# Flags of a chunk-selecting attention: PSUM to the score operands without a DMA between

## The chip, the cores and the metric

The kernel runs on one core of a Trainium2 chip. The time is device microseconds of one launch; the kernel before took 357.41 us (median of 3 runs, 354.07 to 358.31). The profile is of one further execution, whose span from the first to the last instruction is 337.3 us. Engines: PE multiplies matrices and transposes, ACT, DVE and POOL work on vectors, SP issues DMAs. DMAs copy between HBM and SBUF, or from SBUF to SBUF. PE writes to PSUM, which ACT and DVE read.

## The reference

An attention layer that keeps six chunks of keys per query, followed by a dense two-layer network plus a mixture of eight experts, of which each row takes one. Only the attention is touched by the change. Cut:

```python
# q, k, v: (4, 8, 768, 64); chunks of 32 keys, 24 of them
k_min, k_max = min and max of each chunk of k
ub = sum over d of max(q * k_min, q * k_max)          # a bound for each query and chunk
ub = where(chunk not later than the query's own, ub, -1e9)
top_chunks = argsort(ub)[..., -6:]                    # the six chunks kept
scores = q @ k.T / sqrt(64)
scores = where(chunk of the key in top_chunks and key not after query, scores, -1e9)
attn = softmax(scores)
out = attn @ v
# then, on (3072, 512): relu(x @ w1) @ w2, plus gate * relu(x @ w1[e]) @ w2[e] for the row's expert e
```

## The kernel before

Heads are worked on in 16 pairs. A pair's operands of the score matmul are two tiles of K and two of Q, each 128 partitions by 768 positions, in three rotating sets (`NB = 3`). The contraction runs over the 128 partitions, and the mask is folded into it: half of the partitions hold the 64 head dimensions, and part of the other half holds, on K's side, -30000 where a key lies in chunk c (`exf`), and on Q's side a flag that is 1 where the query does not keep chunk c. So the product already contains -30000 for each key that is not selected.

- head 0: `k0[0:64]`, `r0[0:64]` are K and Q; `k0[64:96]`, `r0[64:96]` are chunk table and flags.
- head 1: `k1[64:128]`, `r1[64:128]` are K and Q; `k1[0:32]`, `r1[0:32]` are chunk table and flags.

Rows left over are zero on one side of the product. The steps for one pair, cut:

```python
def prep_k(p):      # transposes of K on PE, ACT copies both heads to k1, chunk max and min on DVE
    pk = pprep.tile([128, S], HF, name="pp")          # PSUM, two buffers shared by all "pp"
    ...
    nc.scalar.copy(k1, pk)                            # L384
    for i, op in enumerate((ALU.max, ALU.min)):
        nc.vector.tensor_reduce(out=ks[:, i], in_=k1 in chunks, op=op, ...)      # L388
    ... kb = ks times masks of the two heads                                     # L391, L393

def prep_kt(p):
    nc.sync.dma_start(out=k0[0:64], in_=k1[0:64])     # L397, K's second copy
    nc.sync.dma_start(out=k1[0:32], in_=exf[0:32])    # L398

def prep_q(p):
    ... transposes of Q to pq (PSUM)                  # L405
    nc.scalar.activation(qp, pq, AF.Relu)             # L408
    nc.vector.tensor_copy(r0, pq)                     # L409, all 128 partitions
    nc.sync.dma_start(out=r1[64:128], in_=r0[64:128]) # L410, Q's second copy

def prep_ub(p):
    ... bounds of all chunks by matmul (PSUM)         # L416, L420
    ... nc.vector.max per 128 queries and head        # L426, the eight largest
    flags = fl[p % 2]...[:, :, :, 0:NC]
    nc.vector.tensor_tensor(flags, ub, sixth largest, ALU.is_lt)                 # L428

def prep_s(p):
    ps = pprep.tile([128, S], HF, name="pp")
    for t in range(NT):
        nc.tensor.transpose(ps[:, t * 128 : (t + 1) * 128], fl[p % 2][:, t], ident)   # L434
    se = ahead.tile([128, S], HF, name="se")
    nc.vector.tensor_copy(se, ps)                     # L436
    r0, r1 = rT[p % NB]
    nc.sync.dma_start(out=r0[64:96], in_=se[64:96])   # L438
    nc.sync.dma_start(out=r1[0:32], in_=se[0:32])     # L439

def scores(p, u):   # 11 units per pair
    sp = psc.tile([128, 512], FP, name="sp")          # PSUM, three buffers
    ... nc.tensor.matmul(sp[...], kT[p % NB][g][...], rT[p % NB][g][...])        # L448
    nc.scalar.activation(ex, sp, AF.Exp, scale=0.125) # L452
    ... on the diagonal: nc.gpsimd.affine_select(ex)  # L454
```

`fl` has 128 columns per block of queries: 24 flags in columns 0 to 23, 24 in columns 64 to 87, the rest zero since the start of the kernel. After the transpose they stand on partitions 0 to 23 (head 1) and 64 to 87 (head 0), which are the partitions where `r1` and `r0` want them.

The loop over pairs calls these steps between the units of earlier pairs (`n1` is the next pair, `n2` the one after it):

```python
if u == 2: prep_s(n1)
if u == 4: prep_k(n2)
if u == 5: prep_q(n2)
if u == 7: prep_kt(n2)
if u == 9: prep_ub(n2)
... fills: parts of the dense network of the batch before (L242 to L331)
... finish: products with V (L467), division by the row sums (L476, L478)
if u == 0: cast_v(n2); load v of pair p + 4; load an expert's weights
if u == 7: cast_qk(p + 3); load k and q of pair p + 5
```

The scheduler orders the instructions of each engine from these calls; it waits wherever one step reads or overwrites what another writes or reads.

Of the kernel before, what the change touches and what calls it, by code (L numbers as in the profile page):

```python
# [10 lines left out]
HF = mybir.dt.float16  # L11
# [6 lines left out]
def kernel(  # L18
# [12 lines left out]
    nc = tc.nc  # L31
    B, H, S, D = q.shape
# [323 lines left out]
    with (  # L356
# [73 lines left out]
        def prep_s(p):  # L430
            s = st[p]
            ps = pprep.tile([128, S], HF, name="pp")
            for t in range(NT):
                nc.tensor.transpose(ps[:, t * 128 : (t + 1) * 128], fl[p % 2][:, t], ident)  # L434
            se = ahead.tile([128, S], HF, name="se")
            nc.vector.tensor_copy(se, ps)  # L436
            r0, r1 = rT[p % NB]
            nc.sync.dma_start(out=r0[64:96], in_=se[64:96])  # L438
            nc.sync.dma_start(out=r1[0:32], in_=se[0:32])  # L439

        def scores(p, u):
            s = st[p]
# [52 lines left out]
        load(2, "v")  # L495
        load(3, "v")
        prep_s(0)
        prep_k(1)
        prep_q(1)
# [22 lines left out]
        for i, (p, u) in enumerate(seq):  # L522
# [4 lines left out]
            if u == 2 and n1 is not None:  # L527
                prep_s(n1)
# [220 lines left out]
```

## Time and profile before

| | |
|---|---|
| time, median of 3 | 357.41 us |
| span of the profiled execution | 337.3 us |
| busy: PE, DVE, ACT, POOL | 244.4, 165.7, 173.6, 154.0 us |
| DMA | 66.23 MB, mean 196 GB/s |
| `rT<-se` (L438, L439) | 32 transfers of 48 KB |
| `kT<-kT` (L397), `rT<-rT` (L410) | 16 each of 96 KB |
| mean granted PE clock | 0.912 |

A line such as `PE sp L448` names the engine, the tile written and the source line. "DMA rT<-se" is a transfer into tile `rT` from tile `se`. SPq is SP's issuing of DMAs. In the list of waits the engine on the left stood idle until the one on the right released it. The granted clock is a share of full speed, and the DMA share is the mean busy share of the 16 DMA engines; it counts packets, which may overlap, and so can pass 1.

### The profile page before, as it was taken

What the parts mean: (1) busy time and instruction counts of PE and PEld (TensorE: products, weight loads), DVE (VectorE), ACT (ScalarE), POOL (GpSimd) and SP (SyncE); (2) the same over time, 40 slices, a digit from 0 to 9 for tenths busy, and PEclk for the clock granted to TensorE, in tenths of its full rate; (3) what the DMA queues carried; (4) which work ended last, traced back from release to release, by engine and by line L of the source; (5) the groups of instructions that cost most, each with busy time, mean ns of one, the idle gap of its engine ahead of it and who ended that gap; (6) DMA issues with size and microseconds to landing.
All of it is one profiled execution on the core that took longest, in us unless ns stands there. A gap on an engine that the chain in (4) does not pass through costs nothing.

```text
span 337.3 us, 7413 instructions
## 1 busy us (share of the span) xinstructions
PE 244.4 (72%) x2615; PEld 156.8 (46%) x2615; DVE 165.7 (49%) x556; ACT 173.6 (51%) x322; POOL 154.0 (46%) x203
## 2 busy tenths in 40 slices
PE   1418727849949859686686696989874998899882
PEld 1316516628616637454453473655441554444441
DVE  5526606527934447494352586237522454444441
ACT  4318707828817737558373664772341444444441
POOL 6635615436323514443424230110446677777753
PEclk9999958769978969799897989899995999999999
DMA  7976989797998798899994897223869578877760
GB/s 202 276 166 157 185 184 192 143 224 178 195 251 209 180 224 188 176 313 198 248 238 132 151 159 249 76 92 106 277 164 293 171 238 233 244 243 257 227 214 0
DMA packets 80499, 66.23 MB, mean 196 GB/s; under 512 B 30222, under 2 KB 73742, under 8 KB 80464
## 3 DMA queue, kind: packets, MB, share of 16 engines
q1 hardware_dynamic: 65280, 37.17, 40.2%
q0 software_dynamic: 15184, 28.60, 37.8%
q8 instruction: 21, 0.34, 0.4%
q14 instruction: 14, 0.11, 0.1%
HBM read 50.62 MB, written 20.91 MB: 212 GB/s over the span
## 4 chain that ended last, share of the span: by engine, by line
DMA 38%; PE 31%; issue 8%; DVE 8%; POOL 6%; ACT 4%; SPq 3%; POOLq 1%; ACTq 0%; DVEq 0%
DMA rT<-se 24%; PE sp L448 10%; DMA xg<-xd,gi 9%; PE yp L326 6%; POOL xg L647 3%; ACT ex L452 3%; DMA kT<-kT 3%; PE hp L317 3%; PE op L467 2%; POOL out_dram L695 2%; PE yp L691 2%; SPq L88 2%; PE hp L674 2%; PE pp L434 1%; DVE ks L388 1%
## 5 line engine op out<-in xcount | busy, mean ns | idle before, releaser
L452 ACT ACTIVATE ex<-sp 128x512 f16<-128x512 f32 (+1 forms) x176 | 92.6, 591 | 66.3 <-PE sp L448 63.0
L448 PE MATMUL sp<-rT,kT 128*128 128x128 f16 (+3 forms) x384 | 72.3, 297 | 46.8 <-DMA rT<-se 45.7
L454 POOL TENSOR_SCALAR_AFFINE_SELECT ex<-ex 128x512 f16<-128x512 f16 x48 | 31.8, 665 | 84.1 <-ACT ex L452 83.8
L448 PEld LDWEIGHTS <-kT 128*128 128x128 f16 x384 | 32.0, 109 | 56.3 <-issue 50.9
L467 PE MATMUL op<-v,ex 128*128 128x65 f16 x672 | 52.2, 201 | 8.0 <-ACT ex L452 4.7
L467 PEld LDWEIGHTS <-ex 128*128 128x128 f16 x672 | 39.7, 103 | 24.0 <-ACT ex L452 8.5
L695 POOL DMA_INDIRECT out_dram<-yo,si x31 | 31.4, 1013 | 16.0 <-DVE yo L694 9.3
L685 ACT COPY ehT<-tp 128x512 f16<-128x512 f16 x31 | 18.1, 585 | 36.9 <-PE tp L683 36.9
L388 DVE TENSOR_REDUCE ks<-kT 128x24 f16<-128x768 f16 x32 | 29.1, 947 | 14.7 <-ACT kT L384 13.9
L647 POOL DMA_INDIRECT xg<-xd,gi x31 | 29.8, 963 | 12.3 <-issue 5.8
L674 PE MATMUL hp<-we,exT 128*128 x124 | 31.8, 379 | 4.6 <-DVE exT L668 3.3
L691 PE MATMUL yp<-we,ehT 128*128 x124 | 32.7, 387 | 0.8 <-ACT ehT L685 0.8
L426 DVE MAX8 m<-pp 128x8 f32<-128x8 f32 (+4 forms) x160 | 16.0, 167 | 29.1 <-PE pp L420 28.9
L668 DVE COPY exT<-tp 128x512 f16<-128x512 f16 x31 | 13.1, 424 | 33.3 <-PE tp L666 33.3
L326 PE MATMUL yp<-wd,hT 128*128 128x512 f16 x96 | 28.9, 427 | 0.7 <-DVE ys L223 0.6
L317 PE MATMUL hp<-xT,wd 128*128 128x384 f16 x128 | 27.0, 330 | 1.1 <-ACT hT L319 0.3
L436 DVE COPY se<-pp 128x768 f16<-128x768 f16 x16 | 8.9, 557 | 37.3 <-PE pp L434 37.3
L694 DVE SCALAR_TENSOR_TENSOR yo<-yp,xg 128x512 f32<-128x512 f32 x27 | 20.3, 751 | 13.8 <-PE yp L691 12.0
L677 ACT ACTIVATE eh<-hp 128x512 f16<-128x512 f32 x31 | 18.5, 597 | 14.1 <-PE hp L674 14.1
L371 POOL CAST q<-qf 128x768 f16<-128x768 f32 x16 | 13.2, 824 | 25.9 <-DMA qf<-in_q_dram 19.0
L319 ACT ACTIVATE hT<-hp 128x384 f16<-128x384 f32 x32 | 15.8, 495 | 13.2 <-PE hp L317 7.5
L376 POOL CAST v<-vf 128x768 f16<-128x768 f32 x16 | 13.2, 827 | 17.5 <-PE op L467 12.8
(123 smaller groups left out, 386.0 us busy)
## 6 DMA issues: line engine op xcount, KB each, us to landing
we<-in_moe_w_dram POOLq DMA_DIRECT2D x16, 512.0 KB, 8.1
kf<-in_k_dram SPq DMA_DIRECT2D x32, 192.0 KB, 4.1
qf<-in_q_dram SPq DMA_DIRECT2D x32, 192.0 KB, 4.5
vf<-in_v_dram SPq DMA_DIRECT2D x32, 192.0 KB, 5.3
xd<-ys SPq DMA_DIRECT2D x24, 256.0 KB, 3.0
xo<-xbig SPq DMA_DIRECT2D x4, 792.0 KB, 6.7
xd<-xbig SPq DMA_DIRECT2D x4, 792.0 KB, 8.0
kT<-kT SPq DMA_DIRECT2D x16, 96.0 KB, 4.6
```

What stands on the lines that cost most here:

```text
L317: nc.tensor.matmul(hp, wd[:, ko, j * 128 : (j + 1) * 128], xT[:, ko, g * G * 128 : (g + 1) * G * 128], start=(ko == 0), stop=(ko == NK - 1))
L326: nc.tensor.matmul(yp, hold["h"][:, j, i * 128 : (i + 1) * 128], wd[:, NK + j], start=(j == 0), stop=(j == NK - 1))
L388: nc.vector.tensor_reduce(out=ks[:, i], in_=kp.rearrange("d (c w) -> d c w", w=32), op=op, axis=mybir.AxisListType.X)
L448: nc.tensor.matmul(sp[:, o : o + w], kT[p % NB][g][:, kt * 128 : (kt + 1) * 128], rT[p % NB][g][:, a * 128 : z * 128], start=(o == 0), sto ...
L452: nc.scalar.activation(ex[:, 0:o], sp[:, 0:o], AF.Exp, scale=0.125)
L454: nc.gpsimd.affine_select(out=ex, in_=ex, compare_op=ALU.is_ge, fill=0.0, base=0, pattern=[[0, 4], [1, 2], [2, 64]], channel_multiplier=-1)
L467: nc.tensor.matmul(s["op", g][:, t * (D + 1) : (t + 1) * (D + 1)], ex[:, o : o + 128], v16[p % NB][:, g, kt, :], start=first, stop=(last_o ...
L647: nc.gpsimd.indirect_dma_start(out=dst, out_offset=None, in_=src, in_offset=bass.IndirectOffsetOnAxis(ap=gi[:, i : i + 1], axis=0))
L674: nc.tensor.matmul(hp, s["xT"][:, ko], wef[:, bass.ds(offs[i] + ko * 512, 512)], start=(ko == 0), stop=(ko == NK - 1))
L691: nc.tensor.matmul(yp, s["hT"][:, j], wef[:, bass.ds(offs[i] + (NK + j) * 512, 512)], start=(j == 0), stop=(j == NK - 1))
L694: nc.vector.scalar_tensor_tensor(o, yp, s["x"][:, Dm : Dm + 2].bitcast(FP), s["y"], ALU.mult, ALU.add)
L695: sc = nc.gpsimd.indirect_dma_start(out=out, out_offset=bass.IndirectOffsetOnAxis(ap=si[:, i : i + 1], axis=0), in_=o, in_offset=None, bou ...
```

## The change

The tile `se` and its two transfers go. DVE copies the transposed flags from PSUM into the two score operands directly, in two instructions of 64 partitions. The copies cover the whole half (64 rows in place of 32); the added rows are the zero columns of `fl`. Only K's second copy, the chunk table and Q's second copy are still moved by DMA. It is meant to take a transfer from SBUF to SBUF, and its latency, out of the way from flags to scores.

```diff
             ps = pprep.tile([128, S], HF, name="pp")
             for t in range(NT):
                 nc.tensor.transpose(ps[:, t * 128 : (t + 1) * 128], fl[p % 2][:, t], ident)
-            se = ahead.tile([128, S], HF, name="se")
-            nc.vector.tensor_copy(se, ps)
             r0, r1 = rT[p % NB]
-            nc.sync.dma_start(out=r0[64:96], in_=se[64:96])
-            nc.sync.dma_start(out=r1[0:32], in_=se[0:32])
+            nc.vector.tensor_copy(r0[64:128], ps[64:128])
+            nc.vector.tensor_copy(r1[0:64], ps[0:64])
```

In the changed kernel the two copies are L436 and L437, and every later line stands two lines higher (the scores are L446).

## The prediction

> **What bounds the kernel now.** I read the page first (shares of busy time, chain that ended last), then the waits, then the chain in order of time, then the stretches. No engine is saturated: PE is busy 72% of the span and every other engine about half. The chain says where the rest goes.
>
> ```profile
> PE 244.4 (72%) x2615; PEld 156.8 (46%) x2615; DVE 165.7 (49%) x556; ACT 173.6 (51%) x322; POOL 154.0 (46%) x203
> ...
> DMA rT<-se 24%; PE sp L448 10%; DMA xg<-xd,gi 9%; PE yp L326 6%; POOL xg L647 3%; ACT ex L452 3%; DMA kT<-kT 3%; PE hp L317 3%; PE op L467 2%; POOL out_dram L695 2%; PE yp L691 2%; SPq L88 2%; PE hp L674 2%; PE pp L434 1%; DVE ks L388 1%
> ```
>
> The first entry of the chain by line, 24% of 337.3 us = 81 us, is the transfer that the change removes: `rT<-se`. The list of waits gives the time in which PE really stood still for it, and what else stood behind it:
>
> ```profile
> ACT ex L452 <- PE sp L448: 63.0, 26, 8.3
> PE sp L448 <- DMA rT<-se: 45.7, 13, 7.3
> DVE se L436 <- PE pp L434: 37.3, 13, 7.6
> POOL q L371 <- DMA qf<-in_q_dram: 19.0, 7, 5.7
> ```
>
> Columns are total us, times, longest. 13 of the 16 head pairs made PE wait, 45.7/13 = 3.5 us each; ACT's 63 us in front of the exponential and DVE's 37 us in front of the `se` copy lie behind the same wait. One turn of the loop in the chain (start, length in us):
>
> ```profile
> 184.74 0.35 PE pp L434 x6
> 185.12 0.56 DVE se L436
> 185.70 5.85 DMA rT<-se
> ...
> 191.69 0.38 PE sp L448 x4
> ```
>
> The flags of pair p+1 are transposed (L434), copied (L436), sent by DMA (L438, L439), and only then can the scores of pair p+1 start (L448). The transposes of p+2 in turn stand in PE's queue behind scores of p+1. So the transfer is in a ring, paid once per pair. Its time from issue to landing:
>
> ```profile
> DMA to landing us min/median/max: 1.9/5.4/10.6
> ```
>
> By stage (columns: length, then busy us and instruction counts of PE, PEld, DVE, ACT, POOL, the granted clock, DMA share, GB/s):
>
> ```profile
> 24.00:207.00 183.00, 134.28 (x1759) 96.43 (x1759) 100.86 (x390) 110.28 (x211) 71.05 (x98) 0.87 0.90 200
> 207.00:225.00 18.00, 15.73 (x155) 9.83 (x155) 5.21 (x14) 12.99 (x27) 3.96 (x6) 0.91 0.22 78
> 225.00:337.00 112.00, 88.62 (x652) 46.29 (x650) 48.19 (x112) 43.64 (x77) 65.18 (x66) 0.97 0.66 205
> ```
>
> Attention proper is 24 to 225 us. In its first 183 us PE is busy 134.3 and idle 48.7, nearly all of it the 45.7 us above. The last 112 us (dense layers of the last batch, then the experts) do not touch the flags: the change can gain nothing there.
>
> [...] the trace has 549 to 559 ns for `se`. [...] The clock here is 0.87 from 24 to 207 us against 0.97 later, with waits up to 7.3 us[...].
>
> **The change, part by part.**
> 1. Removed: 32 transfers `rT<-se`, two per pair. On the path that is the 45.7 us of PE standing still. SP also loses two issues per pair (medians 0.80 and 0.59 us, single ones up to 4.9 us), which lets the remaining transfers start sooner. In bytes it is little: 32 x 48 KB = 1.5 MB of 66 MB, so the DMA engines are hardly relieved.
> 2. Changed: one DVE copy of 128x768 (0.56 us) becomes two of 64x768[...]. DVE gains 16 x 0.55 = 8.8 us, to about 106 + 9 of the 201 us from 24 to 225: not a bound. From last transpose to the first operand ready it is now 0.56 us in place of 0.56 + about 5.9; head 0 needs only the first half.
> 3. Moved: DVE now writes `r0[64:128]`, which the transfer of Q's second copy (L410) reads. So the first half copy must wait for that transfer, and DVE, which works in order, would stand with it. L410 lands in 2.1/4.1/6.6 us (min/median/max). Its source is written by L409, and in the compiled order of the changed kernel the flags copy of the same pair comes about a pair later on DVE, 9 us or so. I count this as mostly hidden, exposed where SP is held up in front of L410 by a load that waits for its buffer.
> 4. Reordered: in the compiled order of the changed kernel PE's flag transposes of the next pair stand behind the second head's first scores, and its scores follow soon after (in early pairs: 6 flag transposes, 6 of K, 7 products with V, then the scores). So the distance from flags to scores is under 1 us of PE work: tight, but about the length of the copy.
>
> What the ring costs without the DMA, from durations in the trace: transposes of K 0.50, ACT's copy 0.80, two reductions 2 x 0.94, Q's copy 0.55, the `kb` products 0.37, bound matmuls 0.70, ten maxima 0.90, the flags 0.45, flag transposes 0.35, two half copies 1.11: 7.6 us, and with 0.1 us for each of ten hand-offs (my allowance) 8.6 us per pair. PE's own work per pair: (134.3 + 15.7) us busy over the 201 us, times the present period of 12.86 us (first L438 at 21.05, last at 213.96, 15 periods) = 9.6 us. ACT: (110.3 + 13.0)/201 x 12.86 = 7.9 us. So PE becomes the bound, at 9.6 us at best.
>
> Nothing here runs in a perfect packing: PE and ACT hand each unit to each other in order with three score buffers, and the batch-end stretches (for example 191.5 to 208.7 us, DVE 13.09 of 17.2 us) are thick with small DVE work. I take PE at 89% busy, a choice between its 96% in the densest stretch (73.0 to 86.5 us: 12.96 of 13.5) and its 73% now: 9.6/0.89 = 10.8 us per pair. That saves 15 x (12.86 - 10.8) = 31 us. Seen from the waits: of 45.7 us about a third comes back as waits on ACT, on DVE and on loads. Before the first scores (23.9 us, which waited for a transfer issued at 21.05) I expect up to 2 us, and take 1 us off again for DVE's extra copies in the batch-end stretches, net 0 to 1. The sum is -30.5: 357.4 - 30.5 = 327 us. The timed median stands 18 us above the profiled execution; I carry the saving over in us, not as a ratio.
>
> **The rivals.**
> A. The DMA engines become the bound. Share 0.90 over 12.86 us is 11.6 us of packets per pair; at the highest share seen for a whole pair, 1.10 (152.9 to 165.9 us), that is 10.5 us, at 1.0 it is 11.6. For: POOL already waits 19 us for loads of Q. Against: those waits are largely early, loads are issued more than a pair ahead, and expert weights can come late without harm. Period 11.6: saving 19 us, about 338.
> B. DVE stands at L436 for L410's transfer, and the removed wait comes back on another engine. If it cost 2 us in each of 15 pairs on top of 10.8: about 357. Against it: the distance of some 9 us. I give it 5%, with part of it (338 to 345) more likely than all.
> C. Clean removal: all of the 45.7 us goes[...]. Period near 9.6: about 308 to 312. For: the idle time has almost no other cause. Against: it supposes that no new wait arises.
> D. A wait hidden already. This would need the DMA to run beside other PE work; PE's 45.7 us of idleness say it does not.
>
> **Range and chances.** 8 in 10 between 313 (close to C) and 341 (A, with some of B). Faster by over 2% means under 350.3 us: only a full B or two partial ones miss it, so 0.93; within 2% 0.05; slower 0.02, for an order of instructions worse than I read it.
>
> **What would show it.** Right: no `rT<-se` anywhere; PE's wait in front of L446 (the scores) falls from 46 us to under 10; the stage ends near 195 us; PE busy above 80% in it; two half copies of about 0.55 us each; PE's clock at or above 0.90 in that stage; the last 112 us unchanged. Step 3 is wrong if DVE's wait in front of L436 names the transfer `rT<-rT`; rival A shows as POOL or PE waiting for `qf`, `kf` or `vf`, with a share at 1.0 or more and a period above 11 us. The prediction as a whole is wrong if PE's waits before the scores stay above 25 us, whatever their releaser.

## The result, and the profile after

The changed kernel took 327.74, 329.05, 332.68 and 339.33 us, the kernel before 357.14 us (median of 4, 354.07 to 358.31). Executions more than 1.5% above the fastest of their kernel, here the last two, are left out of the medians and differences from here on. That gives 328.40 us, 28.7 us less; with all four it is 330.87 us, 26.3 less. The ratio is 0.921, its 95% interval 0.910 to 0.931. The prediction was 327 us, 30.5 less.

The first two lines are the page's busy times and its chain by line, of the changed kernel.

```profile
PE 241.8 (74%) x2615; PEld 156.0 (48%) x2615; DVE 174.0 (53%) x572; ACT 174.8 (53%) x322; POOL 154.7 (47%) x203
...
DMA rT<-rT 22%; PE yp L689 7%; PE hp L672 6%; PE sp L446 5%; PE yp L326 5%; PE hp L317 5%; DVE ks L388 3%; PE op L465 3%; POOL out_dram L693 2%; PE tp L664 2%; DVE rT L436 2%; POOL xg L645 2%; DVE rT L437 2%; DMA xg<-xd,gi 2%; PE tp L681 2%
```

`rT<-se` is gone, and in its place at the head of the chain stands another transfer, `rT<-rT`, with nearly the same share. The list of waits (us in total, times, longest) says who stands for it:

```profile
DVE rT L436 <- DMA rT<-rT: 42.7, 14, 7.7
ACT ex L450 <- PE sp L446: 31.1, 26, 5.2
...
PE sp L446 <- DVE rT L436: 17.8, 8, 5.4
...
PE pp L405 <- DVE rT L437: 11.1, 3, 6.6
```

Before, PE stood 45.7 us for a transfer; now DVE stands 42.7 us for one. PE gets only part of it: 17.8 us in front of the scores, and 11.1 us in front of Q's transposes (L405), whose PSUM buffer is free only when the second half copy (L437) is done. The copies themselves, and Q's transfer (from L410):

```profile
L436 DVE COPY rT<-pp x16: 560/561/561, 20.1 to 187.2; 64x768 f16<-64x768 f16 x16
L437 DVE COPY rT<-pp x16: 540/550/550, 20.7 to 187.8; 64x768 f16<-64x768 f16 x16
```
```profile
DMA to landing us min/median/max: 2.6/4.8/6.9
```

The first starts of L436 at 20.1 and the last at 187.2 us make a period of 167.1/15 = 11.14 us per pair, against 12.86 before. One turn of the new ring, from the chain in order of time (start, length):

```profile
32.42 6.95 DMA rT<-rT
39.37 0.03 issue
...
39.46 0.56 DVE rT L436
40.02 0.03 issue
40.05 0.55 DVE rT L437
40.60 1.72 DVE ks L388 x2
42.32 0.47 DVE rT L409
42.78 0.73 DVE kb L391
43.52 0.04 DVE kb L393
43.56 5.58 DMA rT<-rT
```

Of 11.1 us, 7.0 are the transfer. Nearly all other links of this ring are DVE's, in its own order: the copy that must wait for the transfer (L436) holds up the work that starts the next one. The two `kb` links are none: the transfer reads only `r0`, which L409 had finished at 42.8 us. It was issued at 43.6 because SP was still issuing loads of K.

Stages, from the stretches of both profiles. The attention stage ends with the last division by row sums, at 227.2 us before and at 200.1 us now, 27 us earlier:

```profile
24.00:200.00 176.00, 141.62 (x1925) 101.21 (x1922) 115.04 (x421) 124.14 (x238) 74.88 (x103) 0.93 0.94 208
200.00:327.00 127.00, 92.43 (x629) 48.94 (x626) 47.36 (x111) 42.56 (x75) 65.31 (x66) 0.92 0.56 179
```

From there to the end this execution takes 127 us and the one before took 110. The next section shows that this is not the change: in another execution of the same kernel it is 112 us.

### The profile page after: what moved, and what is told of

It reads as the page before. It is cut to its first block, busy times and chain, and to the rows that moved or that the text cites. A ratio compares the mean times of both kernels' runs of the same rounds, so it can differ in the third digit from the quotient of the medians.

```text
span 327.3 us, 7387 instructions
## 1 busy us (share of the span) xinstructions
PE 241.8 (74%) x2615; PEld 156.0 (48%) x2615; DVE 174.0 (53%) x572; ACT 174.8 (53%) x322; POOL 154.7 (47%) x203
## 4 chain that ended last, share of the span: by engine, by line
PE 39%; DMA 27%; DVE 12%; issue 8%; POOL 4%; ACT 4%; SPq 3%; another core or an unknown queue 1%; POOLq 0%; ACTq 0%; DVEq 0%
DMA rT<-rT 22%; PE yp L689 7%; PE hp L672 6%; PE sp L446 5%; PE yp L326 5%; PE hp L317 5%; DVE ks L388 3%; PE op L465 3%; POOL out_dram L693 2%; PE tp L664 2%; DVE rT L436 2%; POOL xg L645 2%; DVE rT L437 2%; DMA xg<-xd,gi 2%; PE tp L681 2%
## 5 line engine op out<-in xcount | busy, mean ns | idle before, releaser
L446 PE MATMUL sp<-rT,kT 128*128 128x128 f16 (+3 forms) x384 | 70.0, 280 | 22.6 <-DVE rT L436 17.8
L465 PE MATMUL op<-v,ex 128*128 128x65 f16 x672 | 50.5, 201 | 0.5 <-POOL ex L452 0.2
L446 PEld LDWEIGHTS <-kT 128*128 128x128 f16 x384 | 31.0, 104 | 26.2 <-issue 20.1
L672 PE MATMUL hp<-we,exT 128*128 x124 | 33.8, 397 | 9.6 <-DVE exT L666 6.0
L689 PE MATMUL yp<-we,ehT 128*128 x124 | 34.7, 404 | 7.4 <-ACT ehT L683 4.4
L436 DVE COPY rT<-pp 64x768 f16<-64x768 f16 x16 | 9.0, 561 | 44.6 <-DMA rT<-rT 42.7
L692 DVE SCALAR_TENSOR_TENSOR yo<-yp,xg 128x512 f32<-128x512 f32 x27 | 20.2, 750 | 14.5 <-PE yp L689 9.2
L326 PE MATMUL yp<-wd,hT 128*128 128x512 f16 x96 | 26.0, 394 | 0.4
L319 ACT ACTIVATE hT<-hp 128x384 f16<-128x384 f32 x32 | 15.8, 494 | 15.2 <-PE hp L317 10.3
L672 PEld LDWEIGHTS <-exT 128*128 128x128 f16 x124 | 11.5, 100 | 18.7 <-DVE exT L666 6.8
L426 DVE MAX8 m<-pp 128x8 f32<-128x8 f32 (+4 forms) x160 | 15.8, 166 | 8.4 <-PE pp L420 8.4
```

The costliest lines, as they stand in the source:

```text
L326: nc.tensor.matmul(yp, hold["h"][:, j, i * 128 : (i + 1) * 128], wd[:, NK + j], start=(j == 0), stop=(j == NK - 1))
L446: nc.tensor.matmul(sp[:, o : o + w], kT[p % NB][g][:, kt * 128 : (kt + 1) * 128], rT[p % NB][g][:, a * 128 : z * 128], start=(o == 0), sto ...
L465: nc.tensor.matmul(s["op", g][:, t * (D + 1) : (t + 1) * (D + 1)], ex[:, o : o + 128], v16[p % NB][:, g, kt, :], start=first, stop=(last_o ...
L672: nc.tensor.matmul(hp, s["xT"][:, ko], wef[:, bass.ds(offs[i] + ko * 512, 512)], start=(ko == 0), stop=(ko == NK - 1))
L689: nc.tensor.matmul(yp, s["hT"][:, j], wef[:, bass.ds(offs[i] + (NK + j) * 512, 512)], start=(j == 0), stop=(j == NK - 1))
L692: nc.vector.scalar_tensor_tensor(o, yp, s["x"][:, Dm : Dm + 2].bitcast(FP), s["y"], ALU.mult, ALU.add)
```

## The experiments

Times are medians. Each run stands beside runs of the kernel before on its own chip: 338.55 us for runs 1 to 4, 339.09 for 5 to 8, 334.69 for 9 to 12 (of three executions). A difference between runs of two of these groups is therefore known only to about 4 us. The expectations of runs 2 to 4 are counted from the 330.87 us above; of them only the differences can be compared.

| run | us | ratio to before (95%) | first and last flags copy, us | period, us |
|---|---|---|---|---|
| 1 the change again | 312.67 | 0.935 (0.926 to 0.945); of medians 0.924 | 20.5, 185.1 | 10.97 |
| 2 Q direct | 306.19 | 0.906 (0.899 to 0.913) | 15.2, 181.5 | 11.09 |
| 3 Q by DMA, own source | 311.39 | 0.921 (0.914 to 0.928) | 15.2, 183.5 | 11.22 |
| 4 Q's copy sent twice | 322.03 | 0.952 (0.943 to 0.960) | 20.8, 198.8 (of 326.67 us) | 11.87 |
| 5 V in long runs | 308.19 | 0.911 (0.903 to 0.919) | 20.7, 182.3 | 10.77 |
| 6 Q direct, V long | 296.64 | 0.871 (0.864 to 0.879) | 15.7, 172.0 | 10.42 |
| 7 Q and K direct | 290.43 | 0.858 (0.851 to 0.865) | 14.6, 164.6 | 10.00 |
| 8 Q and K direct, V long | 289.12 | 0.852 (0.846 to 0.858) | 14.9, 163.8 | 9.93 |
| 9 K direct | 302.19 | 0.904 (0.893 to 0.915) | 21.9, 175.0 | 10.21 |
| 10 Q and K direct, flags by DMA | 328.67 | of medians 0.982 | 14.8, 202.4 | 12.51 |
| 11 only head 1 direct | 343.73 | 1.021 (0.999 to 1.042) | 15.2, 215.6 | 13.36 |
| 12 only head 0 direct | 320.21 | 0.956 (0.945 to 0.967) | 14.9, 193.8 | 11.93 |

The period is that of the first DVE copy of flags, (last - first)/15, in the profiled execution, which for run 4 took longer than its median. An interval that holds 1 means no difference shown.

**1. The change again.** No edit.

> The changed kernel again, as the base for the other runs of this chip. Theory (the wait moved): DVE's wait in front of the first half copy, for the transfer rT<-rT, is again some 43 us over 14 pairs, the period of the first half copies is about 11.1 us, and the time is 0.92 of the kernel before. Second point: the length of the expert stage (from the first gather of rows, xg, to the end) was 84.6 us in the profile before and 101.4 us in the profile after, though the change doesn't touch it; if that belongs to the single execution, it is a different length here; if the change causes it, it is near 101 us again.

The wait is there again (43.2 us, 14 times), the ratio's interval overlaps the first one's, and the change saves 25.9 us. From the last division by row sums (198.0 us) to the end (309.7) it is 112 us: the change does not make the expert stage long. The kernel before, whose profile is of an execution of 339.06 us, took 354 us or more beside the first measurement, so both kernels took 16 to 19 us longer there than beside run 1. What made them so was not tried.

DVE's wait has two parts. One is the transfer itself, a median of 4.9 us from issue to landing. The other is that SP issues it late. Its source `r0` is ready when L409 ends, but in 7 of the 15 turns after the first the transfer was issued 2.5 to 5.0 us after that, 22.9 us in all. In three of these turns SP stood right before it for K's transfer to land, because the chunk table (L398) overwrites what that transfer reads. One of these three (start, length, and in brackets the idle time before and what ended it):

```profile
162.74 0.47 SPq L397 DMA_DIRECT2D kT<-kT  x1
...
165.48 0.55 DVE L409 COPY rT<-pp 128x768 f16<-128x768 f16 x1
...
168.35 0.56 SPq L398 DMA_DIRECT2D kT<-exf  x1
...
169.00 0.69 SPq L410 DMA_DIRECT2D rT<-rT  x1
...
176.03 0.56 DVE L436 COPY rT<-pp 64x768 f16<-64x768 f16 x1 [3.52 <-DMA rT<-rT]
```

In the other four SP was still issuing loads, K's transfer or results of the dense network. SP's own waits in the whole run have (us in total, times, longest)

```profile
SPq L398 <- DMA kT<-kT: 32.3, 12, 5.0
```

**2. Q direct.** Head 1's Q stands on partitions 64 to 127 of PSUM already; a DVE copy of 64x768 (561 ns in this run) takes the place of the DMA:

```diff
-            nc.sync.dma_start(out=r1[64:128], in_=r0[64:128])
+            nc.vector.tensor_copy(r1[64:128], pq[64:128])
```

> Q's second copy also straight from PSUM by DVE, so no transfer rT<-rT, and one more DVE copy of 0.55 us per pair. Theory (the new bound is DVE standing for that transfer before it may overwrite its source): the wait of 43 us goes, the period falls from 11.1 us to between 9.6 and 10.3 us (PE's own work), 12 to 22 us less than the changed kernel, some 309 to 319 us. Rival 1 (DMA engines are full): only 1.5 MB of 65 MB less, so within 2 us of the changed kernel. Rival 2 (PE and ACT can't pack closer): within 2 us, and their waits on each other grow by what the DVE wait loses.

306.19 us: 6.5 less than run 1, where the theory had 12 to 22. DVE's wait is gone, and the period is still 11.09 us. Of the 6.5 us, 5.3 are the start: the first flags copy need not wait for a transfer and comes at 15.2 in place of 20.5 us. So in the steady part another ring, of nearly the same length, lay behind the wait of 43 us. The waits name it:

```profile
PEld L446 <- DMA kT<-kT: 14.3, 5, 4.7
PE sp L446 <- DMA kT<-kT: 13.5, 5, 4.5
```

This is K's second copy (L397). Its follower, the chunk table (L398), must wait for it in SP's queue, 55.1 us in this run. The chain of run 2 has

```profile
37.19 10.53 DMA kT<-kT
...
47.81 5.22 DMA kT<-exf
```

**3. Q by DMA, from a tile of its own.** The edit keeps the transfer and takes away what waits for its source; DVE does as many copies as in run 2, in nearly the same places.

```diff
-            nc.vector.tensor_copy(r0, pq)
-            nc.sync.dma_start(out=r1[64:128], in_=r0[64:128])
+            s["qq"] = qq = ahead.tile([128, S], HF, name="qq")
+            nc.vector.tensor_copy(qq, pq)
+            nc.vector.tensor_copy(r0[0:64], pq[0:64])
+            nc.sync.dma_start(out=r1[64:128], in_=qq[64:128])
...          the bound matmuls read qq in place of r0
```

> The transfer of Q's second copy stays, with its size and its place, but reads from a tile of its own, so that nothing which DVE writes waits for it; DVE has the same extra copy of 0.55 us as in the run with no such transfer. Theory (it is the wait for the source to come free, not the transfer): the same time as that run within 1.5 us, 309 to 319 us. Rival 1 (the DMA engines or the transfer as such): no gain, about 330 us. Rival 3 (the scores of head 1 need the transfer's data soon after): half the gain, with PE waiting for rT<-qq.

311.39 us: 1.3 less than run 1, whose executions of 311.45 and 313.89 us reach down to it, so no gain is shown; 5.2 more than run 2. The start comes at 15.2 us as in run 2, so it was the busy source that held it. But the wait for the source, taken away alone, gains next to nothing: run 2's gain needs the transfer to be absent, as rival 1 had it. PE has no wait for `rT<-qq` among its longer ones. It stands for K's two transfers 24.4 us in place of 20.3, though K's second copy lands no later than in run 2 (5.9 against 6.4 us, medians). Why is open.

**4. Q's copy sent twice.**

```diff
             nc.sync.dma_start(out=r1[64:128], in_=r0[64:128])
+            nc.sync.dma_start(out=dup[p % NB][64:128], in_=r0[64:128])
```

> The changed kernel with Q's second copy sent twice, the second time to a tile that nobody reads, from the same source; the flags copy then waits for both. Theory: the second lands 0.5 to 1.5 us after the first, so 15 pairs lose 8 to 20 us: 338 to 350 us. Rival 2 (packing of PE and ACT): no change beyond 2 us. Rival 1 (full DMA engines): 16 x 96 KB more of 65 MB, about 2%: at most 4 us more.

322.03 us, 9.4 more than run 1: within the 8 to 20 us of the theory. But its mechanism is not shown: DVE's wait for the second transfer is 35.8 us, no more than run 1's 43.2, although this profile is of a longer execution. The second transfer also takes SP 0.59 us per issue (median) and adds 16 x 96 KB to what the DMA engines move; it lands in 4.8 us (median). That lengthening costs while removing the wait hardly gains would fit two rings of about the same length; run 9 tests that.

**5. V in long runs.** V lands in wrong rows, so this run (and 6 and 8) computes other values; bytes and the order on the compute engines are those of run 1, with 58483 packets in all in place of 78963. SP's order differs in part.

```diff
-nc.sync.dma_start(out=f[:, g], in_=src[b, 2 * hp + g].rearrange("(t p) d -> p t d", p=128))
+nc.sync.dma_start(out=f[:, g].rearrange("p t d -> p (t d)"),
+                  in_=src[b, 2 * hp + g].rearrange("(p t) d -> p (t d)", p=128))
```

> The changed kernel with V loaded in runs of 1536 bytes in place of 256: the same bytes, a sixth of the packets of these loads (24576 packets fewer to 4096), the same order of instructions on the four compute engines; V's rows come out in another order, so the values are not the reference's. Theory A (since the change the DMA engines are full through attention, share 0.95 or more from 24 us on, and the wait of DVE for rT<-rT is mostly how long a transfer takes in full queues): the transfer lands faster than 4.8 us, DVE's wait of 43 us falls to under 25, and the time falls by 8 to 20 us. Theory W (the wait is the order of DVE's work, whatever the DMA load): the wait stays within 8 us of 43 and the time within 3 us of the changed kernel.

308.19 us, 4.5 less than run 1 on another chip, about the size of the uncertainty; DVE's wait is 33.9 us, between the two theories. The median from issue to landing of Q's transfer did not fall (5.1 us, against 4.9 in run 1), so the mechanism that theory A gave is not seen.

**6. Q direct, V in long runs.** Both edits.

> Q's second copy straight from PSUM and V in long runs (values not the reference's, as above). Without the long runs this kernel was 306.19 us, with a period that did not fall although DVE's wait was gone. Theory A: the DMA engines hold it, so it falls by 8 to 20 us, to 286 to 298. Theory K (K's second copy, kT<-kT, is the next wait of the same kind): only as far as that transfer lands sooner, 3 to 6 us. Theory P (PE and ACT packing): within 2 us.

296.64 us, 9.6 less than run 2: within A's range, at its weak end; theory K's 3 to 6 us are exceeded. Runs 7 and 8 decide between them.

**7. Q and K direct.** Run 2's edit and

```diff
-            nc.sync.dma_start(out=k0[0:64], in_=k1[0:64])
-            nc.sync.dma_start(out=k1[0:32], in_=exf[0:32])
+            nc.gpsimd.tensor_copy(k0[0:64], k1[0:64])
+            nc.gpsimd.tensor_copy(k1[0:32], exf[0:32])
```

> As the run with Q direct, and K's second copy and the chunk table copied by GpSimd in place of DMA: no transfer within SBUF is left. Theory K: the 24 us of PE waits for kT<-kT and kT<-exf go, 6 to 12 us faster than 306.2. Theory A: 2.3 MB less of 63 MB and SP no longer held by the wait of its own queue, 2 to 5 us faster. Rival: GpSimd, which also does the casts and the diagonal masks, gets two more copies per pair and delays these: no gain or slower.

290.43 us, 15.8 less than run 2: more than theory K's 6 to 12. No transfer inside SBUF is left, and the period is 10.00 us. This kernel leaves nothing of the computation out, and it beats both kernels of the case.

**8. The same with V in long runs.**

> No transfer within SBUF and V in long runs (values not the reference's). Theory A: against the run with all copies direct again 8 to 20 us less, and the DMA share of the attention stage falls from about 0.95 to below 0.85. Theory P: the same time as the run with all copies direct within 2 us.

289.12 us, 1.3 less than run 7, whose interval of the ratio overlaps: theory A falls. The stretch from 24 to 185 us of run 7, then of run 8 (busy PE, PEld, DVE, ACT, POOL, clock, DMA share, GB/s):

```profile
24.00:185.00 161.00, 143.04 (x1991) 101.70 (x1989) 136.93 (x459) 122.83 (x240) 97.35 (x133) 0.98 0.93 204
```
```profile
24.00:185.00 161.00, 142.44 (x1961) 100.78 (x1960) 137.45 (x452) 121.84 (x239) 95.67 (x130) 0.99 0.86 201
```

The DMA share falls from 0.93 to 0.86 and hardly anything follows. A share of 0.9 or more, which looked like full DMA engines, is no bound here. Taking packets away went with 4.5 and 9.6 us only while the pairs still had to wait for transfers inside SBUF. What it changed for these is not shown.

**9. K direct alone.** The edit of run 7 for K, Q by DMA.

> The changed kernel with K's second copy and the chunk table by GpSimd, Q's second copy still by DMA. Q direct alone left the period at 11.1 us, both direct gave 10.0. Theory (two transfers, each on a ring of about the same length, so that either one alone keeps the period): DVE's wait for rT<-rT stays near 43 us, the period stays at 10.7 to 11.2 us, and the time within 6 us of the changed kernel (310 to 318). Rival (K's transfer was the one that counted, Q's wait is slack): nearly all of the gain, 290 to 298 us.

302.19 us: 10.5 less than run 1, between the two. The period falls to 10.21 us although Q's transfer is there, and DVE's wait for it shrinks without being touched:

```profile
DVE rT L436 <- DMA rT<-rT: 18.6, 9, 7.4
```

With runs 1, 2 and 7 this makes a square: Q alone 6.5, K alone 10.5, both 22.2 us. Both together gain more than the sum, 17.0, by about the uncertainty. K's transfers set the period, Q's the start (21.9 us in run 9, 14.6 in run 7) and little of the period. The expected picture, that either one keeps the period, is wrong for K. DVE's wait for Q's transfer shrinks mainly because SP issues it sooner: with no chunk table to wait for, SP is late by 4.4 us in all after the first turn, against 22.9 in run 1, and never by more than 1.5. The transfer also lands in 4.6 us in place of 4.9 (medians), and the scheduler placed some DVE instructions differently. Which of K's two transfers counts, the copy or the chunk table that waits for it in SP's queue, was not tried apart.

**10. Flags by DMA in the version without other transfers.** The kernel before with the edits of run 7: the change alone taken back.

> K's and Q's copies direct, but the flags again through the tile se and two transfers: the change alone taken back in the version without transfers. Theory (each transfer within SBUF on the ring costs its latency, whichever it is): a period of 12 to 12.8 us, PE waiting 35 to 46 us for rT<-se, 318 to 332 us, so that the change is worth 27 to 40 us here, more than beside the other transfers. Rival (what counts is the number of transfers, not which): close to the runs with two kinds left, 303 to 312 us.

328.67 us, 38.2 more than run 7, within the theory's range; period 12.51 us. PE's matmuls stand for the flags again, a little less than the expected 35 to 46 us:

```profile
PE sp L448 <- DMA rT<-se: 33.4, 11, 7.4
```

So the transfer of the flags costs 38 us when it is the only one, and 25.9 us (338.55 - 312.67) beside the other two: about 12 us of the change's worth were hidden by Q's and K's transfers. And direct copies of Q and K without the change bring 6.0 us of 334.69.

**11. Only head 1 direct, and 12. only head 0 direct.** The other head's flags go by `se` and one transfer:

```diff
# 11                                                 # 12
+ nc.vector.tensor_copy(se[64:128], ps[64:128])      + nc.vector.tensor_copy(se[0:64], ps[0:64])
+ nc.sync.dma_start(out=r0[64:96], in_=se[64:96])    + nc.sync.dma_start(out=r1[0:32], in_=se[0:32])
  nc.vector.tensor_copy(r1[0:64], ps[0:64])            nc.vector.tensor_copy(r0[64:128], ps[64:128])
```

> Half of the change: head 1's flags straight from PSUM, head 0's again by tile and DMA, which on SP's queue waits for rT<-rT. Head 0's scores come first, so PE needs this transfer at once. Theory: PE waits for rT<-se 30 us or more in all, DVE no longer waits for rT<-rT, and nearly all of the gain is gone: 328 to 342 us. Rival (the gain came from the order of instructions or DVE's copies, not from the transfer): 312 to 322 us.

> The other half: head 0's flags straight from PSUM, head 1's by tile and DMA. Head 1's scores come half a pair later, so the transfer lies beside head 0's. Theory: nearly all of the gain stays, 314 to 322 us, with DVE's wait for rT<-rT near 40 us as in the changed kernel. Rival (each transfer costs alike): half of the gain, 325 to 332 us.

Run 11 is 343.73 us: nothing is gained (0.999 to 1.042). Run 12 is 320.21 us, 14.5 less than the kernel before, where run 1 had 25.9: somewhat over half of the gain stays, not nearly all. Head 0's scores come first, and PE stands for its flags; head 1's transfer lies in part beside head 0's scores. PE's wait, in run 11 and then in run 12:

```profile
PE sp L448 <- DMA rT<-se: 47.2, 10, 9.2
```
```profile
PE sp L448 <- DMA rT<-se: 10.0, 6, 4.8
```

Run 12's wait of DVE for `rT<-rT` was 13.6 us, not the 40 expected; there that copy also waits in DVE's order behind the copy to `se`. In both runs the scheduler orders the instructions anew, so they are no pure halves of the change.

## Why the prediction was right, and where it was not

- **The bound and the removed wait (step 1): right.** PE stood for `rT<-se` (43.2 of the 45.7 us fell into the 183 us that the prediction sets them beside); run 10 shows that this transfer carries the cost, and run 11 that head 0's alone undoes the whole gain. Head 1's costs too (run 12).
- **Two half copies at 0.55 us (step 2): right.** 560 and 550 ns; half the partitions cost what all had cost (558 ns). Beforehand that was my estimate; the trace of before has a like pair for ACT only, with different sources (copies of 32x768 825 ns, of 128x768 799 ns, means).
- **DVE behind Q's transfer (step 3): wrong.** "Some 9 us or so", about a pair, was the distance I gave from L409 to the flags copy. In a plain turn of the compiled order there are only the `kb` products, one or two divisions, the ten maxima and the flags between them: by the durations of before about 0.37 + 2 x (0.56 + 0.19) + 0.90 + 0.45 = 3.2 us of DVE work, against a transfer of 4.8. With what else the scheduler put between them in other turns, the profile of run 1 has 4.6 us at the median. I had carried the distance over from the program's loop, where the flag transposes stand a pair later, though step 4 saw that the scheduler had moved them. The exposure that step 3 allowed, SP held up in front of L410, came in 7 of 15 turns of run 1, and was no exception. The wait is 42.7 us, as rival B had it. Rival B's time (357) did not come: B added each stalled microsecond of DVE to the period, while PE stood for DVE's two copies 17.8 + 11.1 us. Removing the wait alone (run 3) shows no gain (1.3 us), and the transfer with it (run 2) gave 6.5, of which 5.3 were the start, since K's ring was about as long.
- **The period: 10.8 predicted, 11.14 and 10.97 measured, by two errors that offset, which is luck.** PE at 89% busy was too much: it is 141.6 of 176 us, 80%, with 34.4 us idle. PE's work per pair at 9.6 us was too much as well: 0.80 x 11.14 = 9.0 us, with the granted clock at 0.93 in place of 0.87. From 24 us to about the last division PE was busy 151.5 us before at a clock of 0.87, 141.6 us after at 0.93, 137.0 us in run 1 at 0.95 and 135.8 us in run 7 at 0.98: less at each higher clock, for 1913 to 1938 matmuls. It stood idle for 51.5, 34.4, 37.0 and 17.2 us of these stretches. Run 1, with more idle time than the first execution, has the higher clock, so the idle time alone does not order them; what raises the clock is not shown.
- **Rival A: wrong.** Its period of 11.6 us did not come with a share of 0.94, and run 8 shows no bound at 0.93. Runs 5 and 6 against 8 (4.5 and 9.6 us for the packets taken away, against 1.3) suggest that here the load matters only through transfers that others wait for.
- **What I did not list: K's second copy.** It was 3% of the chain before, and with the chunk table behind it, it set the period after the change (run 9).
- **Signs.** "Under 10 us" of PE's wait before the scores was wrong: 22.6, of which 17.8 through DVE. That is just under the 25 us that were to refute the whole. The stage end near 195 us came at 200. The last stage was as before in run 1.
- **The sum.** 30.5 us less predicted, 28.7 measured, 25.9 in run 1. The step that failed is the third. The wait that it took as hidden is there, but K's ring, which is not in the sum at all, kept it from costing more than the 6.5 us of run 2.

## What to carry to other kernels

Here a DMA taken off a ring exposed the next one on it (without `rT<-se`, DVE stood 42.7 us for `rT<-rT`; without that too, K's ring kept the period at 11.09 us). So before counting the gain, list every transfer that some engine must wait for per turn, also those that only wait for a source to come free, and what stands ahead of each in the issuing engine's queue. In all three operands producer and consumer stood on the same partitions, and copies by DVE and GpSimd (0.55 to 0.82 us) replaced every transfer; doing this for all three brought 0.858 where the change alone brought 0.924 to 0.935. Read distances from the compiled order of the changed kernel, not from the loop in the source.

## What the runs showed of the hardware

- Two transfers of 96 KB inside one core's SBUF took 4.9 us (Q) and 5.4 us (K) from issue to landing at the median, up to 9.6 us, in run 1 (4.8 and 7.2 us in the first profile); a DVE copy of the same Q rows from PSUM took 0.56 us (run 2), and GpSimd's copy of the same K rows inside SBUF 0.82 us (run 7).
- At a mean DMA share of 0.93 (run 7, 24 to 185 us) the DMA engines were no bound: a quarter fewer packets (75635 to 55155, the edit of run 5) was worth 1.3 us in run 8, which has no transfer inside SBUF.
- GpSimd took on two more copies of 0.82 us per pair, and the whole became faster (306.19 us in run 2, 290.43 in run 7): in run 7 it was busy 97.4 of the 153 us from 24 to 177 us.
- A transfer that had to wait held up those behind it in SP's queue: in run 1 SP stood 32.3 us for K's transfer before the chunk table, and in the turn shown there Q's transfer, whose source was ready at 166.0 us, was issued at 169.0, behind the chunk table (168.4).
